# Moving the output products' sums of two middle groups from VectorE adds to accumulating DMAs, and telling the list scheduler that PSUM banks are read by one engine at a time

## The chip, the cores and the metric

The kernel runs on one core of a Trainium2 chip. The metric is the device time of the whole program in microseconds. Three runs of the kernel before gave 1047.87, 1048.98 and 1049.39 us, with a median of 1048.98 us. Times of a view are microseconds from the start of the profiled span unless marked ns.

## The reference

Three stages follow one another: an attention with a sigmoid in place of the softmax, and two layers of two matrix products each, with an activation between the two.

```python
scores = scale * np.matmul(q, k.transpose(0, 1, 3, 2)) - np.log(S)   # batch 4, 12 heads, S = 448, head size 64
x = np.matmul(1.0 / (1.0 + np.exp(-scores)), v)                       # as 1792 tokens x 768
h = x @ moe_w_in;   g = h - np.tanh(h);                x = g @ moe_w_out     # 768 -> 2048 -> 768
h = x @ moe2_w_in;  g = s * np.maximum(h, 0)**2 + b;   out = g @ moe2_w_out
```

The weights arrive as 64-bit floats, everything else as 32-bit floats. The output is float32, 1792 x 768.

## The kernel before, in words

**Two passes.** The batch of four is worked in two passes of two batch entries (896 tokens); `Layers.sb` is 0 in the first pass and 1 in the second. Each pass has its attention, pair of heads by pair of heads (`prep` L365, `qk` L418, `av` L460), and then the two layers (`Layers.run` L861). The first pass also converts the weights: each 64-bit block is loaded, turned into 32-bit by one scaling and three integer operations (`conv` L585), kept in DRAM for the second pass, and split into a high and a low float32r part (`hi_lo` L628). Every product is made of three float32r products: high by high, low by high, high by low.

**Groups.** A layer has 16 blocks of 128 hidden features, worked in four groups of four (`group` L969, `grp` 0 to 3). A group makes its hidden products as two pairs of blocks, each pair by a scheme of seven products instead of eight (`pair_open` L894, `pair_close` L917), applies the activation (`activated` L761: ScalarE and VectorE), splits the result into high and low (`split` L809), and then makes its share of the output products. In the first pass these are `out1` (L1112, layer 0: 12 results of 128x448 in a group) and `out2` (L1187, layer 1: 14 results of 128x384). Each result is a sum in one PSUM bank over the group's four blocks. The output is the sum over the four groups, held in SBUF in tiles named y.

**The part that the change touches.** `evict` in `out1` (L1135) and in `out2` (L1212) moves a finished bank into y. In group 0 it is a copy that either ScalarE or VectorE may do. In groups 1 to 3 it is a VectorE addition that reads the bank and y and writes y. After it the bank is free. In layer 0, group 3 then makes from y the operands of layer 1 (`half`, `less`: more VectorE work). The second pass uses something else in its groups 0 to 2 (`out_sums` L1002): its `add` (L1039) copies a bank into one of the small tiles t, and a DMA issued from the GpSimd (POOL) queue adds the tile onto a sum in DRAM. The small tiles are ten in the first pass (four, and six more once the attention has ended) and twenty in the second; `Slots.take` and `give` (L217, L220) hand them out in turn.

**What sets the order.** Nothing is issued when it is described. Each operation is put down with `Plan.add` (L102): the engine or engines that may do it, its estimated busy time and, for a DMA, the time until it has landed, and keys that it reads and writes. `Plan.emit` (L122) then simulates the whole kernel: TensorE's order is fixed, as written; each other engine takes, at the earliest simulated time at which an operation of its list is ready, the one that is due first (`chosen` L152), and may hold back for one that is due soon. An operation open to ScalarE or VectorE goes to the engine that reaches it first. An operation is ready once those that it depends on have ended, plus a lag of 0.22 us where they ran on another engine. Two operations that only read the same bank have no dependence on each other in this simulation. The order that results is the program's: on the chip each engine works its list strictly in order.

```python
            def chosen(e, w):
                t = max(free[e], min(ready[k] for k in w))
                now_ = sorted((k for k in w if ready[k] <= t), key=lambda k: (due[k], k))
```

**Reads of a bank in the attention.** `prep` transposes q and k of a pair of heads into one pair of banks; five operations read it: two copies (either engine), and two subtractions and one copy on VectorE. `x_sums` (L518) reads the bank with a pair's attention result three or four times, on either engine.

Of the kernel before, what the change touches and what calls it, by code (L numbers as in the profile page):

```python
# [13 lines left out]
ALU = mybir.AluOpType  # L14
# [5 lines left out]
def tile_kernel(ctx, tc, q, k, v, w_in1, w_out1, w_in2, w_out2, s_in, b_in, out):  # L20
# [17 lines left out]
    B, H, S, D = q.shape  # L38
# [9 lines left out]
    FC = DF // P  # L48
    HM = DM // 2
# [5 lines left out]
    FG = 4  # L55
# [22 lines left out]
    class InOrder:  # L78


        def __init__(self, engine):
            self.engine = engine
# [4 lines left out]
    pe, act, dve, pool, sp = (InOrder(e) for e in (nc.tensor, nc.scalar, nc.vector, nc.gpsimd, nc.sync))  # L87
# [5 lines left out]
    class Plan:  # L93


        LAG = 0.22
        AHEAD = 2.0

        def __init__(self):
            self.ops, self.wrote, self.read = [], {}, {}  # L100

        def add(self, eng, cost, fn, r=(), w=(), o=()):  # L102
            deps = {self.wrote[k] for k in (*r, *w) if k in self.wrote}
            for k in w:
                deps.update(self.read.get(k, ()))
            i = len(self.ops)
            for k in r:
                self.read.setdefault(k, []).append(i)
            for k in w:
                self.wrote[k], self.read[k] = i, []  # L110
            if isinstance(eng, tuple):
                costs = {e: (c, c) for e, c in zip(eng, cost)}
            else:
                costs = {eng: cost if isinstance(cost, tuple) else (cost, cost)}
            starts = set()
            for k in o:
                starts.update(self.read.get(k, ()))
                starts.update({self.wrote[k]} if k in self.wrote else ())
                self.read.setdefault(k, []).append(i)
            self.ops.append((costs, fn, deps | starts, starts - deps))  # L120

        def emit(self):  # L122
            ops, lag = self.ops, self.LAG
            n = len(ops)
            after = [[] for _ in ops]
            for i, (_, _, deps, _) in enumerate(ops):
                for d in deps:
                    after[d].append(i)
            short = [min(c[1] for c in o[0].values()) for o in ops]
            clock, due, soon = 0.0, [1e9] * n, [0.0] * n  # L130
            for i, (costs, _, deps, starts) in enumerate(ops):
                soon[i] = max((soon[d] + (0.0 if d in starts else short[d] + (0.0 if None in costs else lag)) for d in deps), default=0.0)
                if "PE" in costs:
                    due[i] = clock
                    soon[i] = max(soon[i], clock)
                    clock += costs["PE"][0]
            for i in reversed(range(n)):
                for j in after[i]:
                    due[i] = min(due[i], due[j] - short[i] - lag)
            left = [len(o[2]) for o in ops]  # L140
            ready = [0.0] * n
            waiting = {e: [] for e in ("PE", "ACT", "DVE", "POOL", "SP", None)}
            queue = {e: sorted((i for i in range(n) if e in ops[i][0]), key=lambda i: due[i]) for e in ("ACT", "DVE")}
            free = dict.fromkeys(waiting, 0.0)
            for i, o in enumerate(ops):
                if not left[i]:
                    for e in o[0]:
                        waiting[e].append(i)
            pe_order, pe_next = [i for i, o in enumerate(ops) if "PE" in o[0]], 0
            order, begun, late = [], [False] * n, 0.0  # L150

            def chosen(e, w):  # L152
                t = max(free[e], min(ready[k] for k in w))
                now_ = sorted((k for k in w if ready[k] <= t), key=lambda k: (due[k], k))
                if e not in queue:
                    return t, now_[0]
                near, held = queue[e], []
                while near and begun[near[0]]:
                    near.pop(0)
                for k in near[:40]:  # L160
                    if due[k] + late > t + self.AHEAD:
                        break
                    if begun[k] or (k in w and ready[k] <= t):
                        continue
                    r = ready[k] if k in w else max(soon[k] + late, t)
                    held.append((due[k], r))
                for i in now_:
                    end = t + ops[i][0][e][0]
                    if not any(d < due[i] and r < end and d + late < end for d, r in held):
                        return t, i  # L170
                wake = min(r for _, r in held)
                return (t, now_[0]) if wake <= t + 0.01 else (wake, None)

            while len(order) < n:
                best = None
                for e, w in waiting.items():
                    if not w:
                        continue
                    if e == "PE":
                        i = pe_order[pe_next]  # L180
                        if i not in w:
                            continue
                        t = max(free[e], ready[i])
                    else:
                        t, i = chosen(e, w)
                    if best is None or t < best[0]:
                        best = (t, e, i)
                t, e, i = best
                if i is None:
                    free[e] = t  # L190
                    continue
                for x in ops[i][0]:
                    waiting[x].remove(i)
                begun[i] = True
                if e == "PE":
                    pe_next += 1
                    late = max(0.0, t - due[i])
                busy, done = ops[i][0][e]
                free[e] = t + busy
                order.append((i, e))  # L200
                for j in after[i]:
                    same = e in ops[j][0] and len(ops[j][0]) == 1 and e not in ("SP", "POOL")
                    ready[j] = max(ready[j], t if i in ops[j][3] else t + done + (0.0 if same or e is None or None in ops[j][0] else lag))
                    left[j] -= 1
                    if not left[j]:
                        for x in ops[j][0]:
                            waiting[x].append(j)
            for i, e in order:
                ops[i][1](e) if len(ops[i][0]) > 1 else ops[i][1]()
# [17 lines left out]
    EITHER = ("ACT", "DVE")  # L227

    def copy(e, o, t):
        (act.copy if e == "ACT" else dve.tensor_copy)(o, t)  # L230
# [36 lines left out]
    raws, ready, avs, flt = {}, {}, {}, {}  # L267
# [289 lines left out]
    class Layers:  # L557
# [444 lines left out]
        def out_sums(self, layer, grp, n, close):  # L1002
# [106 lines left out]
            prod("3", "a", 1)  # L1109
            to("a", 0, 1, True)  # L1110

        def out1(self, layer, grp, n, close):  # L1112

            final = grp == FC // FG - 1
# [20 lines left out]
            def evict(hd, d):  # L1135
                dm = hd * 3 + d
                t = lambda i: ys_t["y"][dm][:, i]
                yk = [cells(dm * T2 + i * S, S) for i in range(2)]
                for i in range(2):
                    bank = ps[hd, d, i]  # L1140
                    if grp == 0:
                        self.do(EITHER, (0.43, 0.54), lambda e, bank=bank, i=i: copy(e, t(i), self.banks[bank]), r=[("b", bank)], w=yk[i])
                    else:
                        self.do("DVE", 0.54, lambda bank=bank, i=i: dve.tensor_tensor(out=t(i), in0=self.banks[bank], in1=t(i), op=ALU.add), r=[("b", bank)], w=yk[i])
                    self.b.give(bank)
# [7 lines left out]
                if dm % 2 == 0:  # L1153
                    k = self.y_t1 = self.t.take()
# [32 lines left out]
        def out2(self, layer, grp, n, close):  # L1187

            final = grp == FC // FG - 1
            last = T2 // P  # L1190
# [21 lines left out]
            def evict(hd, t):  # L1212
                cs = slice(hd * HM, (hd + 1) * HM)
                zt, bank = (lambda: ys_t["z"][t][:, cs]), ps[hd, t]
                ks = cells(t * DM + hd * HM, HM)
                if grp == 0:
                    self.do(EITHER, (0.38, 0.47), lambda e: copy(e, zt(), self.banks[bank][:, :HM]), r=[("b", bank)], w=ks)
                else:
                    self.do("DVE", 0.47, lambda: dve.tensor_tensor(out=zt(), in0=self.banks[bank][:, :HM], in1=zt(), op=ALU.add), r=[("b", bank)], w=ks)
                self.b.give(bank)  # L1220
                if final:
                    self.do("SP", (0.65, 2.0), lambda: store(self.sb, t, zt(), cs), r=ks)
# [120 lines left out]
```

## Time and profile before

| | |
|---|---|
| median of three runs | 1048.98 us |
| the profiled execution | 1049.52 us |
| its span, first to last instruction | 1047.7 us |
| outside of the span | 1.8 us |
| mean granted TensorE clock | 0.997 of full speed |
| instructions | 15664 |

The span runs in this order: attention of the first pass up to about 89 us, its layer 0 up to about 335, its layer 1 up to about 536, attention of the second pass up to about 615, and its two layers to the end. Nearly all instructions carry one source line, that of the helper that records them, so groups are told apart by the names of the tiles: hs, one and two are PSUM tiles, w the split weights, wf and raw the weights on their way, xo and g the activations, y the sums, t the small tiles, acc the second pass's sums in DRAM. A row such as `PE hs` is a matrix product into hs; PEld is TensorE's weight load, SPq and POOLq are DMA issues. An idle time in square brackets stands with the engine whose work ended it.

### The profile page before, as it was taken

Reading aid. Unit: us, or ns where it says so; the run is one execution under the profiler, and the core shown is the slowest. Engines: PE = TensorE matmul, PEld = TensorE weight load, DVE = VectorE, ACT = ScalarE, POOL = GpSimd, SP = SyncE. Lnnn points to the kernel's source line nnn. Section 1 sums busy time; section 2 is a strip of 40 time slices with the busy share of each in tenths; the row PEclk is TensorE's granted clock in tenths of the full one; section 3 lists DMA queues with packets and bytes.
Section 4 is the critical chain, followed back from the end, with each engine's and each line's share of the span. In section 5 each row is a group of like instructions: output and inputs, shape, how many; then the busy total and the mean of one; then the engine's idle time right before and its main releaser. Section 6 shows DMA issues by size and latency. Waiting matters only on the chain.

```text
span 1047.7 us, 15664 instructions
## 1 busy us (share of the span) xinstructions
PE 1029.9 (98%) x5685; PEld 897.0 (86%) x5685; DVE 901.1 (86%) x1501; ACT 592.3 (57%) x969; POOL 141.7 (14%) x186
## 2 busy tenths in 40 slices
PE   8999999999999999999999999999999999999998
PEld 4556999999997999999975569899999999999998
DVE  4899989999999999999646689798977999898862
ACT  4776556363655665554337767565654466666650
POOL 4220000000000000000312100216160003061600
PEclk9999999999999999999989999999999999999999
DMA  6774376656524567654666103919496019293963
GB/s 155 197 192 136 108 239 175 202 166 226 166 74 123 156 206 215 191 182 166 177 173 167 44 29 107 230 54 225 87 231 201 27 39 229 75 211 83 219 165 106
DMA packets 128749, 161.18 MB, mean 154 GB/s; under 512 B 52736, under 2 KB 101120, under 8 KB 128672
## 3 DMA queue, kind: packets, MB, share of 16 engines
q1 hardware_dynamic: 109472, 131.10, 40.6%
q0 software_dynamic: 18400, 28.88, 15.5%
q8 instruction: 45, 0.74, 0.3%
q10 hardware_dynamic: 800, 0.20, 0.1%
q14 instruction: 32, 0.26, 0.1%
HBM read 99.88 MB, written 60.26 MB: 153 GB/s over the span
## 4 chain that ended last, share of the span: by engine, by line
PE 81%; DVE 15%; issue 2%; ACT 1%; DMA 1%; SPq 0%; ACTq 0%; DVEq 0%
PE hs L85 71%; PE two L85 5%; PE one L85 5%; DVE t L85 4%; DVE w L85 2%; DVE xo L85 2%; DVE wf L85 2%; DVE raw L85 1%; DVE y L85 1%; DVE g L85 1%; DMA wf<-wout 1%; DVE kt L85 1%; DVE qt L85 1%; ACT t L85 0%; DVE one L85 0%
## 5 line engine op out<-in xcount | busy, mean ns | idle before, releaser
L85 PE MATMUL hs<-xo,w 128*128 128x448 f32 x2016 | 422.3, 368 | 1.3 <-ACT t L85 0.6
L85 PEld LDWEIGHTS hs<-xo,w 128*128 128x128 f32 x2016 | 377.3, 188 | 39.7 <-ACT t L85 2.1
L85 PE MATMUL hs<-w,g 128*128 128x384 f32 x1290 | 227.8, 334 | 1.3 <-DVE w L85 1.2
L85 PE MATMUL hs<-g,w 128*128 128x448 f32 x1098 | 228.3, 367 | 0.4 <-DVE w L85 0.3
L85 PEld LDWEIGHTS hs<-w,g 128*128 128x128 f32 x1290 | 224.2, 188 | 2.8 <-DVE w L85 1.4
L85 PEld LDWEIGHTS hs<-g,w 128*128 128x128 f32 x1098 | 206.1, 188 | 19.5 <-DVE w L85 0.6
L85 ACT CAST w<-wf 128x768 fp32r<-128x768 f32 (+1 forms) x179 | 138.9, 783 | 116.2 <-DVE wf L85 89.8
L85 DVE TENSOR_TENSOR w<-wf,w 128x768 fp32r<-128x768 f32 (+1 forms) x216 | 187.7, 882 | 16.8 <-PE hs L85 11.2
L85 ACT COPY t<-hs 128x448 f32<-128x448 f32 (+2 forms) x200 | 101.1, 518 | 103.7 <-PE hs L85 99.5
L85 POOL DMA_DIRECT2D acc<-t x106 | 93.3, 1186 | 318.0 <-ACT t L85 108.3
L85 DVE TENSOR_TENSOR g<-t,g 128x448 fp32r<-128x448 f32 (+2 forms) x170 | 98.9, 597 | 7.6 <-ACT g L85 7.0
L85 ACT CAST g<-t 128x448 fp32r<-128x448 f32 (+1 forms) x149 | 81.2, 552 | 31.5 <-DVE t L85 29.8
L85 DVE TENSOR_TENSOR wf<-wf 128x384 f32<-128x384 f32 x168 | 93.2, 555 | 3.7 <-DMA win<-wf 0.4
L85 POOL DMA_DIRECT2D rawqkv<-in_v_dram x36 | 23.0, 644 | 492.7 <-DVE t L85 435.2
L85 ACT ACTIVATE af<-two,nlogs 128x896 f32<-128x896 f32 (+1 forms) x96 | 85.5, 920 | 5.2 <-PE two L85 3.3
L85 DVE TENSOR_TENSOR t<-hs,t 128x448 f32<-128x448 f32 x114 | 70.4, 619 | 7.0 <-PE hs L85 4.1
L85 DVE TENSOR_TENSOR y<-hs,y 128x448 f32<-128x448 f32 (+1 forms) x92 | 52.4, 588 | 16.2 <-PE hs L85 16.0
L85 DVE SCALAR_TENSOR_TENSOR raw<-raw 128x768 uint32<-128x768 uint32 x64 | 61.2, 957 | 3.0 <-ACT raw L85 1.0
L85 DVE TENSOR_TENSOR t<-t 128x448 f32<-128x448 f32 (+1 forms) x98 | 58.8, 603 | 3.8 <-ACT t L85 3.5
L85 ACT ACTIVATE raw<-raw 128x768 f32<-128x768 f32 x61 | 56.3, 923 | 10.0 <-DMA raw<-in_moe_w_in_dram 8.9
L85 ACT ACTIVATE t<-t,b_sb,s_sb 128x448 f32<-128x448 f32 x64 | 48.1, 761 | 23.9 <-DVE t L85 23.7
L85 DVE SCALAR_TENSOR_TENSOR wf<-raw 128x768 uint32<-128x768 uint32 x64 | 60.8, 954 | 0.6
(79 smaller groups left out, 706.7 us busy)
## 6 DMA issues: line engine op xcount, KB each, us to landing
raw<-in_moe_w_in_dram SPq DMA_DIRECT2D x32, 768.0 KB, 5.6
raw<-in_moe_w_out_dram SPq DMA_DIRECT2D x32, 768.0 KB, 6.0
win<-wf SPq DMA_DIRECT2D x32, 384.0 KB, 2.7
wout<-wf SPq DMA_DIRECT2D x32, 384.0 KB, 6.2
wf<-win SPq DMA_DIRECT2D x32, 384.0 KB, 4.4
wf<-wout SPq DMA_DIRECT2D x32, 384.0 KB, 6.2
acc<-t POOLq DMA_DIRECT2D x51, 224.0 KB, 8.1
acc<-t POOLq DMA_DIRECT2D x55, 192.0 KB, 8.1
```

The lines of the kernel that those rows point to most:

```text
L85: return lambda *a, **kw: tc.keep_in_program_order(getattr(self.engine, name)(*a, **kw))
```

## The change

It has two parts. In the first pass, `evict` of groups 1 and 2 copies the bank into a small tile t (ScalarE or VectorE), and a DMA issued from POOL adds the tile onto y in SBUF. Groups 0 and 3 stay as they are, and so does the second pass. And `Plan` keeps, for each PSUM bank, which engine other than TensorE used it last and when that ended; another engine can begin an operation on that bank 0.12 us after that at the earliest. This holds for the whole kernel, the attentions and the second pass included. No operation but the evictions is added or taken away by it; it alters only which engine takes an operation that is open to two, and the order on ScalarE and VectorE, and with it on the DMA queues.

```diff
@@ class Plan
+        TURN = 0.12
@@ Plan.add
             self.ops.append((costs, fn, deps | starts, starts - deps))
+            self.banks.append(() if "PE" in costs else {k for k in (*r, *w) if k[0] == "b"})
@@ Plan.emit
+            def from_(k, e):
+                return max([ready[k], *(last[b][1] + self.TURN for b in self.banks[k] if last.get(b, (e,))[0] != e)])
+
             def chosen(e, w):
-                t = max(free[e], min(ready[k] for k in w))
-                now_ = sorted((k for k in w if ready[k] <= t), key=lambda k: (due[k], k))
+                can = {k: from_(k, e) for k in w}
+                t = max(free[e], min(can.values()))
+                now_ = sorted((k for k in w if can[k] <= t), key=lambda k: (due[k], k))
...
-                    if begun[k] or (k in w and ready[k] <= t):
+                    if begun[k] or (k in w and can[k] <= t):
                         continue
-                    r = ready[k] if k in w else max(soon[k] + late, t)
+                    r = can[k] if k in w else max(soon[k] + late, t)
...
                 free[e] = t + busy
+                last.update((b, (e, t + busy)) for b in self.banks[i])
@@ class Layers
+        def add_on(self, bank, m, to, keys):
+
+            k = self.t.take()
+            self.do(EITHER, (0.43, 0.54) if m == S else (0.38, 0.47), lambda e: copy(e, self.tt[k][:, :m], self.banks[bank][:, :m]), r=[("b", bank)], w=[("t", k)])
+            self.do("POOL", (1.0, 7.0), lambda: pool.dma_start(out=to(), in_=self.tt[k][:, :m], accum_op=ALU.add), r=[("t", k)], w=keys)
+            self.t.give(k)
@@ out1, evict (out2 alike, with HM, zt and ks)
+                    elif not self.sb and 0 < grp < FC // FG - 1:
+                        self.add_on(bank, S, lambda i=i: t(i), yk[i])
                     else:
                         self.do("DVE", 0.54, lambda bank=bank, i=i: dve.tensor_tensor(out=t(i), in0=self.banks[bank], in1=t(i), op=ALU.add), r=[("b", bank)], w=yk[i])
                     self.b.give(bank)
```

## Rows read from the trace of the kernel before

**Rows 1.** Page, busy time of each engine: us, share of the span, instructions.

```profile
PE 1029.9 (98%) x5685; PEld 897.0 (86%) x5685; DVE 901.1 (86%) x1501; ACT 592.3 (57%) x969; POOL 141.7 (14%) x186
```

**Rows 2.** Windows: length; busy us (instructions) of PE, PEld, DVE, ACT, POOL; clock, DMA.

```profile
40.00:89.00 49.00, 45.01 (x369) 24.46 (x366) 44.00 (x82) 34.61 (x51) 9.41 (x15) 1.00 0.62 170
...
160.00:256.80 96.80, 96.80 (x478) 89.40 (x477) 95.80 (x150) 47.49 (x72) 0.00 (x0) 1.00 0.65 199
...
314.00:338.00 24.00, 21.84 (x102) 18.55 (x102) 23.86 (x41) 13.51 (x23) 0.00 (x0) 1.00 0.38 109
...
390.00:480.00 90.00, 90.00 (x491) 87.08 (x490) 88.64 (x140) 46.10 (x67) 0.00 (x0) 1.00 0.61 191
...
536.00:550.00 14.00, 11.59 (x71) 7.18 (x73) 7.98 (x13) 6.67 (x9) 1.90 (x3) 0.76 0.57 133
...
657.00:839.00 182.00, 181.97 (x880) 164.97 (x880) 156.39 (x266) 102.38 (x185) 42.35 (x48) 1.00 0.63 150
```

**Rows 3.** Timeline of PE, first pass, layer 0 into layer 1.

```profile
256.68 22.05 PE L85 MATMUL hs<-xo,w 128*128 128x448 f32 x108
278.57 2.59 PE L85 MATMUL hs<-g,w 128*128 128x448 f32 x12
...
311.40 3.20 PE L85 MATMUL hs<-xo,w 128*128 128x448 f32 x15
314.88 4.53 PE L85 MATMUL hs<-xo,w 128*128 128x448 f32 x21 [0.28 <-ACT t L85]
319.73 9.35 PE L85 MATMUL hs<-xo,w 128*128 128x448 f32 x44 [0.32 <-ACT t L85]
329.38 5.95 PE L85 MATMUL hs<-xo,w 128*128 128x448 f32 x28 [0.30 <-DVE xo L85]
335.17 0.34 PE L85 MATMUL hs<-w,g 128*128 128x384 f32 x1
336.66 1.51 PE L85 MATMUL hs<-w,g 128*128 128x384 f32 x5 [1.15 <-DVE w L85]
338.01 3.88 PE L85 MATMUL hs<-xo,w 128*128 128x448 f32 x18
```

**Rows 4.** Chain that ended last, in order of time: start, us, what.

```profile
88.90 167.35 PE hs L85 x827
...
337.73 198.76 PE hs L85 x1071
```

**Rows 5.** Groups of VectorE in 160 to 262 us: busy, mean ns, idle before.

```profile
L85 DVE TENSOR_TENSOR y<-hs,y 128x448 f32<-128x448 f32 x24 | 14.2, 617 | 0.1
...
L85 DVE CAST w<-wf 128x768 fp32r<-128x768 f32 x2 | 1.1, 554 | 0.0
```

**Rows 6.** Instructions of tile y: duration ns min/median/max, first and last start.

```profile
L85 ACT COPY y<-hs x24: 467/483/537, 127.1 to 370.2; 128x384 f32<-128x384 f32 x13, 128x448 f32<-128x448 f32 x11
...
L85 DVE COPY y<-hs x2: 551/584/616, 132.5 to 368.4; 128x448 f32<-128x448 f32 x1, 128x384 f32<-128x384 f32 x1
```

**Rows 7.** Instructions of tile acc (second pass): POOL's issues, and DMAs' landing.

```profile
L85 POOL DMA_DIRECT2D acc<-t x106: 850/1121/2546, 652.1 to 995.2; - x106
...
DMA to landing us min/median/max: 1.9/7.3/13.4
```

**Rows 8.** Waits of VectorE and of ScalarE, 0 to 90 us: total, times, longest.

```profile
DVE t L85 <- ACT kt L85: 4.6, 7, 0.9
...
ACT y L85 <- DVE xo L85: 2.9, 2, 1.6
```

**Rows 9.** Timeline, start of the second pass's attention.

```profile
538.69 0.53 ACT L85 CAST kt<-two 128x448 fp32r<-128x448 f32 x1 [2.56 <-DVE qt L85]
...
541.07 1.03 PE L85 MATMUL two<-t 64*64 64x224 f32 x8 [2.41 <-DVE kt L85]
```

**Rows 10.** Timeline of PE, second pass, layer 0.

```profile
671.41 22.48 PE L85 MATMUL hs<-xo,w 128*128 128x448 f32 x108
693.74 2.02 PE L85 MATMUL hs<-g,w 128*128 128x448 f32 x9
```

More of the change, by code (lines that the diff above doesn't have):

```diff
@@ L97, in tile_kernel @@
         AHEAD = 2.0
+        TURN = 0.12
         def __init__(self):
-            self.ops, self.wrote, self.read = [], {}, {}
+            self.ops, self.banks, self.wrote, self.read = [], [], {}, {}
         def add(self, eng, cost, fn, r=(), w=(), o=()):
@@ L149, in emit @@
             pe_order, pe_next = [i for i, o in enumerate(ops) if "PE" in o[0]], 0
-            order, begun, late = [], [False] * n, 0.0
+            order, begun, late, last = [], [False] * n, 0.0, {}
+            def from_(k, e):
+                return max([ready[k], *(last[b][1] + self.TURN for b in self.banks[k] if last.get(b, (e,))[0] != e)])
             def chosen(e, w):
-                t = max(free[e], min(ready[k] for k in w))
-                now_ = sorted((k for k in w if ready[k] <= t), key=lambda k: (due[k], k))
+                can = {k: from_(k, e) for k in w}
+                t = max(free[e], min(can.values()))
+                now_ = sorted((k for k in w if can[k] <= t), key=lambda k: (due[k], k))
                 if e not in queue:
@@ L1217, in evict @@
                     self.do(EITHER, (0.38, 0.47), lambda e: copy(e, zt(), self.banks[bank][:, :HM]), r=[("b", bank)], w=ks)
+                elif not self.sb and 0 < grp < FC // FG - 1:
+                    self.add_on(bank, HM, zt, ks)
                 else:
```

## The prediction

> **What bounds the kernel now.** I read the page's busy times first. TensorE is busy for 1029.9 of 1047.7 us [rows 1], so all time in which it stands still is 17.8 us, and no change to another engine can bring more than that and what a stop costs besides. VectorE is next with 86%. So the question is where TensorE stops, and whether VectorE is the cause there. The windows answer it [rows 2]. In the middle groups of layer 0 (160 to 256.8) and of layer 1 (390 to 480), first pass, TensorE is busy all the time although VectorE is at 99% and 98%: VectorE is full there, but not late. Late it is in one place, 314 to 338, the end of layer 0, where TensorE has 21.84 of 24 us. The other stops are in the attentions: 4.0 us idle between 40 and 89, and 2.4 us between 536 and 550, where the granted clock is also 0.76 in the mean, so part of that stretch ran at the lower of its two levels.
>
> The chain of waits says the same. It runs over TensorE alone from 88.90 for 167 us and again from 337.73 for 199 us [rows 4]; the 81 us between are nearly all VectorE's, one operation behind the other. The timeline of TensorE gives the price [rows 3]. The 108 products of 448 columns from 256.68 to 278.57 took 21.89 us, 202.7 ns each. From 311.40 to 338.01 the same number (15+21+44+28) and six of 384 columns took 26.61 us. At the earlier pace they need 21.89, and the six, by their columns, 6 x 0.174 = 1.04. So 3.7 us are lost in this stretch.
>
> A second reading of the same view: the 108 like products of the second pass, from 671.41 to 693.74 [rows 10], took 22.33 us, 206.8 ns each at a full granted clock [rows 2]. TensorE has two paces, 4.1 ns apart, and the slower one is seen after stops. I have no cause for it and only count with it below.
>
> **Part one, the evictions.** Removed: 24 VectorE additions in layer 0 (2 groups of 12) and 28 in layer 1 (2 groups of 14). In layer 0 one takes 617 ns [rows 5], 24 of them 14.8 us. In their place stand as many copies, open to both engines. The like copies of group 0 went to ScalarE 24 times and to VectorE twice [rows 6], so I take 22 of 24 for ScalarE; VectorE is rid of 22 x 0.617 = 13.6 us before its chain of 81 us begins, or little after. That is worth what of it VectorE can use to work ahead. Its bounds are nothing, if the stretch after 257 makes VectorE late by its own work alone, and 3.7 us, the whole loss. I take 3.5: between 160 and 262 VectorE did few copies that ScalarE could have done (2 large ones [rows 5], and one or two small), so it had hardly any slack and ran behind what its buffers allow; 13.6 us is nearly four times the loss.
>
> In layer 1, 28 x 0.55 = 15.4 us (VectorE's copy of that width took 551 ns [rows 6]) also leave VectorE, and I cost that at nothing: TensorE is busy for 90.00 of 90.00 us there [rows 2], so there is nothing to win.
>
> Added: some 48 copies on ScalarE at 0.5 us [rows 6], 24 us in all. In layer 0 that is 22 x 0.53 = 11.7 us on top of 47.5 in 96.8 [rows 2], or 61%; ScalarE's own slack hides it, and if that were gone each would hold a bank for 0.5 us. Then 52 issues on POOL at 1.1 us [rows 7]: POOL does nothing at all in these stretches [rows 2], so no queue stands behind it. The transfers, 24 x 224 and 28 x 192 KB, add 5.4 MB in some 97 us, 55 GB/s to 199 [rows 2]; the second pass ran its accumulating DMAs beside weight loads at 0.63 of the DMA engines without a stop of TensorE between 657 and 839 [rows 2]. Nobody waits for a sum soon: the next group's eviction of the same cells comes some 55 us later, against a landing of 7.3 us and at most 13.4 [rows 7].
>
> The one resource that the evictions newly hold is the small tile, from the copy until the DMA has landed: 0.5 + 1.1 + 7.3 = 8.9 us typically, 15 at most. There are ten, in turn. By the order of the takes the tightest is the last eviction of a group: its tile is wanted again as the tenth after it, when the next group has done seven of its nine-matmul products, 63 x 0.203 = 12.8 us later. So 3.9 us are to spare in the typical case, and I cost this at nothing; bounds: nothing, and the rival below.
>
> **Part two, the banks' turns.** Two engines do take turns on a bank on the chip, though the list knew nothing of it: in the first attention VectorE's copy out of the transposes' bank waited 4.6 us in seven places for ScalarE's copy into kt, and ScalarE's copy into y waited 2.9 us in two places for VectorE's read of the same result [rows 8]. Each engine works strictly in order, so whatever stood behind waited too. With the turns in the simulation such a wait is filled, or the reader chosen otherwise.
>
> In the first attention the bounds are 4.0 us, all of TensorE's idle time between 40 and 89, and a loss of 2, half of that again, as any new order can also stop TensorE; I take a gain of 1.5, since about as much again of the waits is not about turns but about VectorE's load (44.0 of 49 us [rows 2]). At the start of the second attention ScalarE stood idle for 2.56 us until VectorE had read the bank, and TensorE then waited 2.41 for VectorE's last read [rows 9]. The bounds are nothing and 2.4 plus the lost clock, at most 0.24 x 14 = 3.4, so 5.8. But five reads of one bank stay in series and make most of that wait whatever the order, so I take 1.0, and none of the clock. Elsewhere no bank is read by both engines without one needing the other's result, and I take nothing; bounds are 1 us either way.
>
> **The sum.** 3.5 + 1.5 + 1.0 = 6.0 us from the profiled execution's 1049.5 gives 1043.5; the median of the runs is 0.5 below that execution, so 1043.0. A measurement of this kernel tells about 0.2%, 2.1 us, from no change.
>
> **Rival: nothing that counts.** If the loss at 314 to 338 comes from the 81 us of VectorE's chain alone, or the copies go to VectorE after all (same 0.54 us each in the list), part one is worth 0 to 1; with part two at 0 to 1 the time is 1047 to 1049. For it speaks that group 3 also makes layer 1's operands on VectorE; against it, VectorE's full load before 257 and the split of 24 to 2. Chance 0.16.
>
> **Rival: much more.** The stop at 541 shortens enough that the clock holds (2.4 + 3.4), all of the first attention's 4.0 comes back, and the second pass's layer 0 keeps the fast pace for its 880 matmuls (880 x 4.1 ns = 3.6 us [rows 2, 10]): with part one 16.9, or 1032; with two of the three some 1036. Chance 0.17 for under 1039.5.
>
> **Rival: slower, through the small tiles.** If landings come at 16 us instead of 7.3, the last tile of a group is late by 0.5 + 1.1 + 16 - 12.8 = 4.8 us; the copy into it holds the engine's whole queue, banks stay full, and TensorE has 12 matmuls of cover, 2.4 us. Four groups at 2.4 us are 9.6; the stops also bring the slow pace to what is left of layer 0, from about 215 on some 500 matmuls, 2 us. So 1043.0 + 11.6 = 1054.6. It decides from a landing of about 14 us on. Against it: landings of 7.3 us with POOL's issues at 1.1 us in the second pass [rows 7]; for it: VectorE was less full there (156 of 182 us) than it is here [rows 2], and the longest issue took 2.5 us. With new orders that stop TensorE elsewhere I give 0.12 to slower by over 0.2%.
>
> POOL's issues in [rows 7] spread from 0.85 to 2.5 us, so something does hold them at times. The Trainium skill, page "SBUF — State Buffer", section "SBUF: two separate sides", has a rule against this change: a DMA issued from GpSimd has its descriptors written there, and a VectorE copy in a two-port mode locks GpSimd out of the port that it needs, so that the transfer seems blocked. Its measured case went from 620 to 3100 ns, and by that ratio the estimate would be this rival's time or worse. Of that rule the trace shows the sign only: issues went to three times the shortest, not five.
>
> **How the numbers follow.** The forecast case, 1039.5 to 1046.9, has 0.55, the three rivals 0.16, 0.17 and 0.12. Faster by over 0.2% is 0.55 + 0.17 = 0.72, no change 0.16, slower 0.12. The range from 1036 to 1050 leaves out the last part of the larger gain and the slower case.
>
> **What would show it.** Right: additions hs,y fall from 92 to 40 and some 48 copies t<-hs appear on ScalarE; POOL has 52 issues in the first pass; the chain stays on TensorE through 257 to 338 without the stops of [rows 3]; ScalarE's wait for VectorE at the start of the second attention [rows 9] is shorter. Wrong: stops of TensorE behind a copy that waits for a DMA; the stops at 314 to 338 still there with an idle VectorE before them; new stops in an attention.

## The result, and the profile after

The changed kernel takes 1054.39 us (median of six runs, 1050.86 to 1056.24) against 1048.42 of the kernel before in the same runs (1046.08 to 1049.39): a ratio of 1.0059, 95% interval 1.0040 to 1.0079. It is slower. The profiled execution took 1054.52 us, its span 1052.7.

The windows of the changed kernel, in the columns of [rows 2], with two short stretches more:

```profile
40.00:89.00 49.00, 48.55 (x389) 26.80 (x387) 47.53 (x88) 36.53 (x53) 9.22 (x15) 1.00 0.62 166
160.00:256.80 96.80, 96.04 (x470) 87.74 (x469) 86.01 (x130) 53.53 (x87) 20.05 (x23) 1.00 0.88 239
180.00:200.00 20.00, 20.00 (x100) 18.54 (x99) 15.33 (x22) 10.26 (x17) 8.12 (x10) 1.00 1.06 264
314.00:338.00 24.00, 23.25 (x112) 20.35 (x112) 23.90 (x42) 12.91 (x22) 0.00 (x0) 1.00 0.29 92
390.00:480.00 90.00, 85.22 (x454) 81.91 (x453) 77.00 (x116) 46.66 (x74) 20.82 (x24) 0.96 0.82 216
400.00:420.00 20.00, 20.00 (x117) 20.00 (x117) 14.36 (x21) 10.01 (x18) 8.83 (x10) 1.00 1.07 268
536.00:550.00 14.00, 11.75 (x83) 10.12 (x82) 8.81 (x15) 7.03 (x9) 1.92 (x3) 0.92 0.55 135
```

The same two short stretches of the kernel before:

```profile
180.00:200.00 20.00, 20.00 (x101) 18.53 (x100) 19.65 (x31) 6.89 (x10) 0.00 (x0) 1.00 0.59 196
400.00:420.00 20.00, 20.00 (x117) 20.00 (x116) 19.86 (x32) 8.01 (x11) 0.00 (x0) 1.00 0.76 236
```

Three things are to be read. The first attention is better by 3.5 us (TensorE busy for 48.55 us where [rows 2] have 45.01). The end of layer 0, for which the evictions were moved, seems better by 1.4 (23.25 for 21.84), but this window says little: the kernel before had 23.94 in it in a second execution (the last experiment), which came to the end of layer 0 some 3 us later. And layer 1's middle groups, where TensorE had never stopped, lose 4.8 us (85.22 of 90) while VectorE is idle for 13 of the 90. The share of the DMA engines beside the accumulations is 1.06 and 1.07, where it stood at 0.59 and 0.76. (It is the time that the packets took, added up; over 1 they overlapped.)

TensorE's timeline of the changed kernel has the stops one by one (the last bracket of a row is the idle time before it and what ended it). Between 160 and 560 us the seven with a bracket are all; 333.54 answers to 336.66 in [rows 3], 546.53 to the TensorE row of [rows 9], and the other five are new:

```profile
205.93 14.98 PE L85 MATMUL hs<-xo,w 128*128 128x448 f32 x72 [0.68 <-ACT t L85]
...
333.54 1.51 PE L85 MATMUL hs<-w,g 128*128 128x384 f32 x5 [0.57 <-DVE w L85]
...
434.39 17.03 PE L85 MATMUL hs<-xo,w 128*128 128x448 f32 x72 [4.78 <-DVE t L85]
451.26 1.21 PE L85 MATMUL hs<-w,g 128*128 128x384 f32 x6
...
488.74 3.87 PE L85 MATMUL hs<-xo,w 128*128 128x448 f32 x18 [0.76 <-DVE t L85]
492.99 13.04 PE L85 MATMUL hs<-xo,w 128*128 128x448 f32 x63 [0.37 <-DVE t L85]
...
506.27 2.09 PE L85 MATMUL hs<-xo,w 128*128 128x448 f32 x9 [0.25 <-DVE t L85]
...
546.53 0.61 PE L85 MATMUL two<-t 64*64 64x224 f32 x8 [2.25 <-DVE kt L85]
```

The longest stop costs more than its 4.78 us. In the window around it the granted clock is 0.83 in the mean, so part of it ran at the lower of its two levels (columns of [rows 2]):

```profile
420.00:440.00 20.00, 15.22 (x67) 13.62 (x66) 15.87 (x25) 6.41 (x11) 3.48 (x4) 0.83 0.94 268
```

The 72 products behind the stop took 16.87 us (434.39 to 451.26), where 206.8 ns each make 14.89: another 2.0 us.

What the longest stop stands behind is in the chain of waits of the changed kernel, followed back from 520 us (start, us, what):

```profile
408.66 1.48 SPq L85
410.18 12.79 DMA wout<-wf
423.06 0.97 DVE wf L85
424.04 5.96 DMA win<-wf
430.03 0.57 DVE wf L85
...
434.39 48.91 PE hs L85 x253
```

A converted weight block is stored for the second pass; the store takes 12.79 us, VectorE's next conversion waits for the slot it empties, the store of that block takes 5.96, VectorE's sums within the block wait for it, and they and the splits come too late for TensorE. In the kernel before a store of the first kind landed in about half the time. The landing of the stores wout<-wf issued between 400 and 432 us, first of the kernel before (three of them), then of the changed one (two):

```profile
DMA to landing us min/median/max: 5.7/6.8/7.0
```

```profile
DMA to landing us min/median/max: 12.3/12.5/12.8
```

The weight loads raw<-in_moe_w_out_dram of the same stretch went from a median of 5.8 us to 11.8, the stores win<-wf from 2.7 to 5.9. So the theory to test, T1: **the accumulating DMAs fill the 16 DMA engines, and the weights' loads and stores behind them make VectorE late.** Its rivals: T2, the new order is worse by itself; T3, what goes by the number of DMAs and not by their volume (POOL's writing of descriptors, the turn of the small tiles).

### The profile page after: what moved, and what is told of

Its sections match the earlier page's. It is cut to its first block, busy times and chain, and to the rows that moved or that the text cites. A ratio compares the mean times of both kernels' runs of the same rounds, so it can differ in the third digit from the quotient of the medians.

```text
span 1052.7 us, 15841 instructions
## 1 busy us (share of the span) xinstructions
PE 1032.8 (98%) x5685; PEld 897.6 (85%) x5685; DVE 892.5 (85%) x1479; ACT 601.5 (57%) x991; POOL 187.2 (18%) x238
## 4 chain that ended last, share of the span: by engine, by line
PE 70%; DVE 20%; DMA 5%; issue 2%; ACT 1%; SPq 0%; DVEq 0%; ACTq 0%
PE hs L85 57%; PE two L85 7%; PE one L85 6%; DVE t L85 6%; DVE wf L85 4%; DVE w L85 3%; DVE raw L85 3%; DVE g L85 2%; DMA win<-wf 1%; DMA wout<-wf 1%; DMA raw<-in_moe_w_out_dram 1%; DVE xo L85 1%; DMA wf<-wout 1%; DVE y L85 1%; ACT t L85 0%
## 5 line engine op out<-in xcount | busy, mean ns | idle before, releaser
L85 DVE TENSOR_TENSOR w<-wf,w 128x768 fp32r<-128x768 f32 (+1 forms) x216 | 187.8, 883 | 22.5 <-PE hs L85 16.4
L85 ACT COPY t<-hs 128x448 f32<-128x448 f32 (+2 forms) x239 | 120.0, 515 | 121.1 <-PE hs L85 113.1
L85 POOL DMA_DIRECT2D y<-t x52 | 45.8, 981 | 372.7 <-ACT t L85 177.2
L85 ACT CAST g<-t 128x448 fp32r<-128x448 f32 (+2 forms) x144 | 78.5, 552 | 32.6 <-DVE t L85 31.2
L85 ACT ACTIVATE t<-t,b_sb,s_sb 128x448 f32<-128x448 f32 x64 | 48.0, 761 | 26.6 <-DVE t L85 26.4
L85 PE MATMUL two<-qt,kt 64*128 64x448 f32 x414 | 55.5, 390 | 1.6 <-ACT kt L85 1.1
```

Of the source, the lines that this page charges most:

```text
L85: return lambda *a, **kw: tc.keep_in_program_order(getattr(self.engine, name)(*a, **kw))
```

## The experiments

All ratios are to the kernel before on the same chip, in the same rounds, with 95% intervals.

**The turns alone** (`e1_turns_only`) and **the evictions alone** (`e2_evictions_only`):

```diff
-                    elif not self.sb and 0 < grp < FC // FG - 1:
+                    elif False:
...
-                elif not self.sb and 0 < grp < FC // FG - 1:
+                elif False:
```

```diff
-                return max([ready[k], *(last[b][1] + self.TURN for b in self.banks[k] if last.get(b, (e,))[0] != e)])
+                return ready[k]
```

> The changed kernel with the evictions put back as VectorE adds: the banks' turns alone. Theory T1 (the accumulating DMAs crowd the weight loads and stores; the turns are a gain): the first attention keeps its 3.7 us, the stops at 206, 434 and 488 us are gone, the stops at 314 to 338 come back in some form; 1048.4 - 3.7 - 1 = 1043 to 1045.5 us. Rival T2 (the new list is worse in the layers by its order, whatever the transfers): stops of TensorE in the first pass's layers remain, 1048 us or more.

> The changed kernel with the scheduler blind to the turns, as before: the evictions alone. T1: the first attention is as before, the stops in the middle groups of the first pass stay, in all some 5 to 9 us slower than before: 1053 to 1058 us. T2: the layers are as before or better, 1045 to 1049 us.

The turns alone took 1044.66 us, 0.9983 (0.9969 to 0.9997); the evictions alone 1056.55, 1.0095 (1.0070 to 1.0119). Both fit T1. The turns are a small gain by themselves, and all the loss is the evictions'. With the turns alone the middle groups of layer 1 have no stop (TensorE 90.00 of 90), and with the evictions alone the old list too stops there, at 442 us for 2.74 and at 496 for 1.29. That speaks against T2; the thin adds below settle it.

**The same DMAs with an eighth of the bytes** (`e3_thin_adds`; seven eighths of the sums of groups 1 and 2 are left out), and **with the same bytes, not accumulating** (`e4_plain_copies`; the addition is left out). The order is that of the changed kernel in both:

```diff
-lambda: pool.dma_start(out=to(), in_=self.tt[k][:, :m], accum_op=ALU.add)
+lambda: pool.dma_start(out=to()[:, :m // 8], in_=self.tt[k][:, :m // 8], accum_op=ALU.add)
```

```diff
-lambda: pool.dma_start(out=to(), in_=self.tt[k][:, :m], accum_op=ALU.add)
+lambda: pool.dma_start(out=to(), in_=self.tt[k][:, :m])
```

> The changed kernel with each accumulating DMA cut to an eighth of its columns (the rest of the sums of groups 1 and 2 is left out); the order on every engine is the same, and so are the number of DMAs, POOL's issues, the copies and the turn of the small tiles. T1: the weight loads and stores land in their old times (about 6 us instead of 12), the stops at 206, 434 and 488 us go, and the kernel is faster than before: 1048.4 - 3.7 - 1.2 - 3 = 1039 to 1043 us. T2, and rival T3 (POOL's descriptor writing or the small tiles hold things up, which goes by the number of DMAs): the stops stay, 1052 us or more.

> The changed kernel with the DMAs of the two groups as plain copies of the same bytes over the sums, not accumulating (the addition is left out); same order. T1 in the form that an accumulating DMA costs the DMA engines more than its bytes: packets take less time than 141 ns in the mean, the share of the DMA engines falls under 1, stops shrink by half or more, 1042 to 1049 us. T1 in the form that the bytes alone count: as the changed kernel, 1052 to 1056 us.

Thin, the kernel took 1041.96 us, 0.9955 (0.9937 to 0.9973). The copies, the issues on POOL (856 to 1205 ns in layer 1, 856 to 1202 in the changed kernel), the small tiles and every engine's order were the same; only the transfers were short. The windows of 390 to 480 us, of the thin adds:

```profile
390.00:480.00 90.00, 90.00 (x490) 86.81 (x489) 82.68 (x125) 50.42 (x81) 24.40 (x28) 1.00 0.76 214
```

No stop, and the stores beside them land at a median of 6.8 us again. That is T1, and against T2 and T3.

The plain copies did as well, 1041.22 us, 0.9956 (0.9942 to 0.9970), with all the bytes. Why is in the page's queue lines (packets, MB, share of 16 engines), first of the kernel before, then of the changed one, then of the plain copies:

```profile
q0 software_dynamic: 18400, 28.88, 15.5%
```

```profile
q0 software_dynamic: 25888, 39.89, 21.8%
```

```profile
q0 software_dynamic: 21728, 39.89, 18.6%
```

The accumulations add 7488 packets, the plain copies of the same 11.0 MB 3328. By the shares, the accumulations hold all 16 engines for 0.218 x 1052.7 - 0.155 x 1047.7 = 67 us, 1.29 us each; the plain copies for 0.186 x 1041.6 - 162.4 = 31, 0.6 us each. So the first form of T1 holds: the price of an accumulating DMA on the engines is twice that of its bytes. Its sign of shorter packets did not come (150 ns for one of the plain copies, 143 for one of the accumulations): the plain copies need fewer packets, of 3.3 KB in the mean and not 1.5. Whether the addition itself or the smaller packets make the price isn't separated. Beside the plain copies the share was 0.97 and 0.96 in the two short stretches, and the stores landed at a median of 8.1 us. POOL's issues were shorter there too, 537 ns for 858 in the median, but the thin adds had the long ones without harm.

**By layer** (`e7_layer0_only`, `e8_layer1_only`; the condition of one `evict` set to False, the turns kept):

> The changed kernel with the evictions by DMA in layer 0 only, the turns kept. T1: layer 0 has the relief it was meant for (the stops at 311 to 334 shrink) against one stop near 206 and the slower pace behind it; about the turns alone, 1043.5 to 1047 us. If layer 0 bears half of the harm: 1049 to 1051.

> The changed kernel with the evictions by DMA in layer 1 only, the turns kept. T1: 14 accumulations in some 22 us instead of 12, VectorE with nothing to gain, and the stops at 434 and 488 us: 6 to 9 us over the turns alone, 1050.5 to 1054 us. If layer 0 bears half of the harm: 1047 to 1049.

Layer 0 only: 1044.69 us, 0.9981 (0.9967 to 0.9996), as the turns alone. Layer 1 only: 1049.55, 1.0031 (1.0018 to 1.0044), 0.5% over the turns alone. So most of the harm sits in layer 1. TensorE's timelines say so more directly. Layer 0 is counted here from the 132 products hs<-g,w that begin near 116 to 120 us to the end of the six of 384 columns, its last stretch from the 108 products near 311 to the same end, and layer 1 from there to its last 138 products hs<-w,g (us):

| trace | layer 0 | its last stretch | layer 1 |
|---|---|---|---|
| before | 217.8 | 26.6 | 169.3 |
| before, once more | 220.2 | 25.5 | 169.4 |
| turns alone | 218.4 | 26.5 | 169.3 |
| changed | 218.6 | 24.8 | 178.1 |
| changed, once more | 223.7 | 25.3 | 177.4 |
| layer 0 only | 221.6 | 26.0 | 169.3 |
| layer 1 only | 218.4 | 26.9 | 177.6 |
| thin adds | 216.6 | 25.7 | 169.2 |
| plain copies | 216.6 | 25.7 | 169.4 |
| six adds | 216.8 | 25.7 | 169.3 |
| twelve adds | 216.7 | 25.7 | 169.4 |

Layer 1 takes 169.2 to 169.4 us in every one of these traces without its accumulations at full size, and 177.4 to 178.1 with them. In layer 0 all twelve per group gained nothing: what they take off the last stretch is lost before it, at stops near 206 us (0.68, 3.26 and 2.24 us in the three traces) and to the slower pace of [rows 10] behind them. That layer 0 only has the median of the turns alone all the same isn't explained by its trace, which is 3.2 us behind at the end of layer 0. The rows of layer 1's end, of the kernel before and of the changed one (338.01 in [rows 3] and 334.89 are its begin):

```profile
507.35 24.09 PE L85 MATMUL hs<-w,g 128*128 128x384 f32 x138
```

```profile
254.32 22.48 PE L85 MATMUL hs<-xo,w 128*128 128x448 f32 x108
...
334.89 3.87 PE L85 MATMUL hs<-xo,w 128*128 128x448 f32 x18
...
512.98 24.09 PE L85 MATMUL hs<-w,g 128*128 128x384 f32 x138
```

The expected 1050.5 was a little high, and the two parts, -0.02% and +0.48%, fall short of the +0.76% that both together cost over the turns alone; the intervals reach over most of that gap.

**Fewer and farther apart** (`e5_six_adds`, `e10_twelve_adds`: layer 0, second half of the columns only, in group 2 or in groups 1 and 2, where two results end every 4.9 us):

```diff
-                    elif not self.sb and 0 < grp < FC // FG - 1:
+                    elif not self.sb and grp == 2 and hd:
```

> The turns, and accumulating DMAs for only six evictions: layer 0, group 2, second half of the columns, where two come every 4.9 us and not every 2.4. T1 (the DMA engines' time is the price): weight loads in that stretch land in 6 to 8 us instead of 12, no new stop, and VectorE's 3.7 us of relief take part of the stops at 311 to 334: between the turns alone (1044.7) and the thin adds (1042.0), ratio to before 0.995 to 0.998. T2 (any eviction by DMA upsets the in-order lists): 1046 us or more, ratio over 1.000.

> The six adds' rule for both middle groups of layer 0 (second half of the columns, two every 4.9 us): twelve accumulations. T1: spread like this they do not crowd the loads, so no stop in layer 0 before 310 us; as the six adds or a little better, 1040 to 1042 us, ratio 0.993 to 0.996. If the relief is used up by the six already: the same as six within 0.1%. If the number in a layer counts and not how close they come: stops near 206 or 260 us as in layer 0 alone, 1043.5 us or more.

Six took 1041.11 us, 0.9949 (0.9936 to 0.9963), the best here and faster than both kernels; twelve took 1041.97, 0.9954 (0.9938 to 0.9970), the same. Neither stops TensorE in layer 0 before 311 us, and the weight loads raw<-in_moe_w_out_dram beside the accumulations land at a median of 5.5 us with six and of 8.0 and 8.2 with twelve, where the changed kernel has 11.6 and 10.0 in the two groups. Six came out a little under the forecast, which put the thin adds (1042.0) as the lower end. Of the 0.34% between the six and the turns alone (3.6 us), the stretch that was to be relieved shows only a part, 0.8 us by the table above. Their two traces are 2.5 us apart: another 0.8 lies before 116 us, and 0.8 in layer 0 ahead of the stretch, where the trace of the turns alone fell to the slower pace from 253 us on. What of this comes back in every execution isn't shown.

**The list told of the longer landings** (`e9_list_told`):

```diff
-self.do("SP", (3.9, 5.3), lambda: sp.dma_start(out=raw_w[k]
+self.do("SP", (3.9, 11.5), lambda: sp.dma_start(out=raw_w[k]
...
-self.do("SP", (1.9, 3.0), fn, r=[("f", k)], w=[("d", key)])
+self.do("SP", (1.9, 10.0), fn, r=[("f", k)], w=[("d", key)])
```

> The changed kernel with the list told of the landings that were measured under the accumulations: 11.5 us for a weight load in place of 5.3, 10 for a store in place of 3.0; nothing else. If the harm is that the list expects the transfers too soon (VectorE's strict order then stands behind a late one while other work is ready): the stops at 434 and 488 us shrink by half or more, 1044 to 1049 us. If it is that the DMA engines are full, and VectorE has nothing else to do: the stops stay, 1052 to 1057 us.

1057.45 us, 1.0100 (1.0076 to 1.0124). The time is that of the second case, even a little over it, but the sign is that of the first: the stops at 434 and 488 nearly went (0.43 and 0.59 us are left near 500), and others came where no accumulation runs, among them 148 (1.16), 315 to 343 (eight, 4.4 in all), 356 (1.04) and 397 (0.69 and 0.54), presumably since the list now thinks every transfer slow. Whether a list that knew it of those stretches alone would keep the gain stays open.

**The additions on POOL itself** (`e6_pool_adds`):

```diff
-self.do("POOL", (1.0, 7.0), lambda: pool.dma_start(out=to(), in_=self.tt[k][:, :m], accum_op=ALU.add), r=[("t", k)], w=keys)
+self.do("POOL", (1.0, 1.0), lambda: pool.tensor_tensor(out=to(), in0=self.tt[k][:, :m], in1=to(), op=ALU.add), r=[("t", k)], w=keys)
```

> The changed kernel with the 52 additions done by POOL itself, from the small tile onto y in SBUF, in place of DMAs. T1: no transfer is added, so the weight loads land in their old times and the stops in the middle groups go: 1040 to 1045 us. Rival: POOL's own additions are so long (several us each), or hold up VectorE's instructions so much, that VectorE loses what it was relieved of: instructions of VectorE in 180 to 260 us longer by tenths of a us, 1047 us or more.

1072.10 us, 1.0243 (1.0229 to 1.0257): the rival was right. VectorE's groups between 160 and 262 us of this kernel (the columns of [rows 5]) show it:

```profile
L85 DVE SCALAR_TENSOR_TENSOR wf<-raw 128x768 uint32<-128x768 uint32 x16 | 20.3, 1279 | 0.2
L85 DVE TENSOR_TENSOR w<-wf,w 128x768 fp32r<-128x768 f32 x17 | 19.2, 1136 | 0.0
...
L85 DVE TENSOR_SCALAR raw<-raw 128x768 uint32<-128x768 uint32 x15 | 12.1, 807 | 0.0
```

In the kernel before the same three are:

```profile
L85 DVE TENSOR_TENSOR w<-wf,w 128x768 fp32r<-128x768 f32 x20 | 18.9, 950 | 0.1
...
L85 DVE SCALAR_TENSOR_TENSOR wf<-raw 128x768 uint32<-128x768 uint32 x16 | 15.2, 954 | 0.2
...
L85 DVE TENSOR_SCALAR raw<-raw 128x768 uint32<-128x768 uint32 x17 | 9.4, 554 | 0.0
```

All three work on SBUF alone, and they grew in the mean by a third, a fifth and nearly a half. A copy out of a bank did not: within eight additions of POOL on end (first row) VectorE's kept its 0.61 us, while the conversion before it took 1.91:

```profile
240.77 13.92 POOL L85 TENSOR_TENSOR y<-t,y 128x448 f32<-128x448 f32 x8 [34.31 <-ACT t L85]
...
243.82 1.91 DVE L85 SCALAR_TENSOR_TENSOR wf<-raw 128x768 uint32<-128x768 uint32 x1
245.65 0.61 DVE L85 COPY t<-hs 128x448 f32<-128x448 f32 x1
```

The Trainium skill, page "SBUF — State Buffer", section "Who interferes with whom", has VectorE's second pair of SBUF ports shared with GpSimd as an exclusive lock, taken by VectorE's two-input instructions against a GpSimd instruction that reads SBUF. The two-input rows agree. The shift raw<-raw, with one input, grew as well, which these words alone don't cover.

**Both kernels once more** (`e11_before_again`, `e12_after_again`; no edit, one execution each):

> The kernel before, profiled once more, to see what differs between executions of one program. If the pace of TensorE after a stop is a matter of chance, the stretch of the second pass's layer 0 takes 202.7 ns a product here or 206.8, with the same stops before it; the stops of the first attention and at 314 to 338 us are the program's and return within 0.3 us each. If the pace follows the program, it is as in the first profile everywhere.

> The changed kernel, profiled once more. T1: the weight stores and loads beside the accumulations land in about 12 us again and TensorE stops near 434 and 488 us again, 4 to 7 us in all there; the stop near 206 again. If those stops were an accident of one execution, they are somewhere else.

The changed kernel's stops came back: 2.22 us at 208, 3.87 at 438, 0.95 at 492, with the stores of that stretch landing at a median of 13.0 us. They are the program's. The kernel before had its stops of the first attention again within 0.03 us (0.91, 0.63 and 1.32 before the products with v). Of the stops at 314 to 338 only the last did as expected, 1.16 us for 1.15; the three of 0.28 to 0.32 are not there (315.40 below, against 311.40 of [rows 3]), and the stretch took 25.5 us and not 26.6. And its pace was another. Its timeline, to be held against 256.68 of [rows 3] and 671.41 of [rows 10]:

```profile
259.60 22.48 PE L85 MATMUL hs<-xo,w 128*128 128x448 f32 x108
281.92 2.64 PE L85 MATMUL hs<-g,w 128*128 128x448 f32 x12
...
315.40 22.83 PE L85 MATMUL hs<-xo,w 128*128 128x448 f32 x108
...
339.57 1.51 PE L85 MATMUL hs<-w,g 128*128 128x384 f32 x5 [1.16 <-DVE w L85]
340.92 3.81 PE L85 MATMUL hs<-xo,w 128*128 128x448 f32 x18
...
672.63 22.05 PE L85 MATMUL hs<-xo,w 128*128 128x448 f32 x108
694.52 1.99 PE L85 MATMUL hs<-g,w 128*128 128x448 f32 x9
```

22.32 us, the slow pace, in the first pass, and 21.89, the fast one, in the second: the reverse of the first execution, with the same program.

## Why the prediction was wrong

**The step that failed** is the sentence that costs the transfers at nothing: 5.4 MB in each layer in some 97 us, 55 GB/s to 199. It counted bytes where the DMA engines' time counts, and spread them over 97 us where they come in bursts. Twelve accumulations at 1.29 us are 15.5 us of all engines, within the 23 us in which POOL issued them (178.8 to 201.4): 0.69 on top of the 0.59 that were there. What the runs showed in place of nothing: stores of converted weights in 12.5 us and not 6.8, VectorE waiting for them, and 8 us (0.76%) lost against the turns alone. The page of the kernel before had the price: 15.5% of 1047.7 us for 28.88 MB, of which the second pass's accumulations are 22.5, is 5.6 us of all engines per MB, 62 us for 11 MB. The second pass was no comparison either: its 0.63 is a mean over 182 us, and two stretches in it stand at 1.08 and 1.05, without a stop of TensorE:

```profile
760.00:780.00 20.00, 20.00 (x99) 18.16 (x98) 17.46 (x29) 12.26 (x22) 14.95 (x17) 1.00 1.08 222
780.00:800.00 20.00, 20.00 (x99) 18.16 (x98) 13.53 (x22) 11.20 (x20) 0.86 (x1) 1.00 1.05 276
```

So a share over 1 does not stop TensorE by itself; in layer 1 it did, since a chain of work waited for what came late. In the second pass the weights are only loaded, not loaded, converted and stored; that this is the difference wasn't tested.

**Layer 1, "nothing to win" costed at nothing.** Right as to the gain, and that was the point to stop at: a stretch with no stop of TensorE has only something to lose, and most of the loss is there, 8 to 9 us of layer 1 in the traces.

**The gain of 3.5 us at 314 to 338** was too high, by the term that lets nearly all of VectorE's relief come back as time. The stretch took 24.8 and 25.3 us in the two executions of the changed kernel, 26.6 and 25.5 in those of the kernel before. VectorE was relieved much as worked out: its additions of results to the sums, y<-hs,y, went from 92 to the expected 40, and of the copies to small tiles ScalarE took 39, not 48 (its group t<-hs from 200 to 239). But the layer's last group, from its 108 products near 256 us to the end of the six, took the kernel before 81.3 us in both executions, at the fast pace and at the slow one, and 80.6 and 81.3 in the changed kernel; with the thin adds, which have the relief and not the harm, 80.4. So it is VectorE's own chain of 81 us that sets this time, which was the condition of the first rival (nothing that counts), and the relief before it was worth 0.9 us against the kernel before and 1.6 against the turns alone (82.0).

**The turns.** The mechanism was right: VectorE's wait in the first attention for ScalarE's copy into kt fell from 4.6 us in seven places to 1.9 in one. The gain of 1.5 there was too low, the profile has 3.5; at the second attention the wait of 2.41 became 2.25 and not 1.4. By the runs the turns are worth 0.17%, 1.8 us (0.3 to 3.2), against 2.5 in the sum; why the 3.5 of the profile, which came back in both executions, do not show in full isn't known.

**The slower rival had the time, 1054.6, and not the reason.** That it came within 0.2 us of the measured 1054.4 is luck. The accumulations land in 3.6 to 12.1 us in layer 0 and 4.1 to 11.7 in layer 1, under the 14 from which the small tiles were to decide, and no copy of the first pass waits for one. POOL's issues took 0.85 to 1.35 us, less than in [rows 7], and the thin adds, as many, did no harm: the rule on blocked descriptors (the Trainium skill, page "SBUF — State Buffer", section "SBUF: two separate sides"), which I had placed there, does not make this loss.

**The paces.** I charged the slow pace to stops. The two executions of one program say otherwise: with the same stops behind them, the last at 85 us, they went through the first pass's layer 0 from 120 us on at 202.7 ns (but for one stretch) and at 206.7. 4.1 ns on 880 products is 3.6 us, so it can make up much of the 1042.9 to 1051.5 us over which the kernel before was measured. A difference between two single traces is no better than that.

## What to carry to other kernels

Cost a DMA that is to relieve an engine by the time it holds the DMA engines (the page's share of a like queue, per MB), within the burst in which it comes, and add the share that the stretch already has; over 1, expect the transfers that share the engines to land late, and look for the work that waits for them. Relieve an engine only where its lateness shows as a stop of the bound engine: six of the fifty-two evictions, with the turns, had all of the gain that was found, and those of layer 1, where nothing had stopped, brought most of the loss. And test volume and order apart: the same list with thin transfers tells them apart in one run.

## What the runs showed of the hardware that was not expected

An accumulating DMA from SBUF onto SBUF held the 16 DMA engines for 1.29 us, by the page's share, where a plain copy of the same bytes held them for 0.6; the 52 went out in 7488 packets against 3328. TensorE's product of 448 columns runs at 202.7 or 206.8 ns at the same granted clock, for hundreds of products on end, and which of the two is not fixed by the program.
